# Spacing a router's serial search wider along a stream of matmuls

## The chip, the cores and the metric

The kernel runs on one core of one Trainium2 chip. The metric is the device time of one execution in microseconds (us). TensorE (PE) multiplies, VectorE (DVE), ScalarE (ACT) and GpSimd (POOL) do the elementwise work, and transfers are issued from the queues of SyncE (SP), ScalarE and GpSimd.

## What is computed

Attention over four batches of 576 tokens gives 2304 rows of 512 values. A dense layer follows, and then a mixture of eight experts in which each expert takes exactly 288 tokens, chosen greedily by descending gate value:

```python
a = x @ w1; b = x @ w2
x = (a * b @ w3) @ w_out                  # 2304 x 512
logits = x @ w_gate                       # 2304 x 8
order = np.argsort(-logits.flatten())     # greedy: best pairs of token and expert first
for idx in order:                         # skip a token that has an expert, an expert with 288 tokens
    ...
for e in range(8):
    h = np.maximum(x[mask_e] @ w1[e], 0)  # 512 -> 1024
    out[mask_e] = h @ w2[e]               # 1024 -> 512
```

Products run as three passes over a high and a low part of each operand (hh, hl, lh), so each product of the formula is three matmuls.

## The kernel before

The order on every engine is the order in which the program emits instructions; no scheduler reorders them. An engine works through its instructions in that order and stops at the first whose operands are not there. Four stages follow each other: attention with the first dense products (to about 304 us), the product w3 @ w_out (`make_w`, 8 tiles of 8 groups), x2 (`make_x2`, 18 chunks of 128 tokens, 8 groups each), and the experts.

Routing runs through the last three. It doesn't need x2, since the gate is folded into earlier weights. It has seven rounds; each round finds, by a search in six steps, the threshold at which some expert is full, gives that expert its tokens, and closes it. A step is a chain from engine to engine: VectorE compares all gate values with 40 trial thresholds (`Gt`, L808), TensorE counts with 18 small matmuls (L822) against a comparison matrix `CR` that ScalarE copies in two parts ahead of each round (L790), and VectorE picks the threshold (L824 to L827). Ahead of each round and behind it stand some 25 small VectorE operations and one pair of matmuls (L838, L840). After round k the index of the full expert (`wi`) is ready, and `make_list(k)` makes that expert's token list while round k+1 runs; its matmuls (L729, L730, L749) and routing's share one PSUM bank (tag `rt`).

`routing()` and the stream of other matmuls (`filler()`: x2, then the experts) are two generators. Where routing yields, it names how many ns it wants filled. The loop at the end gives the stream that many ns times a pace, and the stream pays per yield: 680 for three matmuls of 512 columns in x2, 395 for three of 288 columns in the experts. The pace is PACE0 while the stream is in x2 and PACE1 once it is in the experts. What a yield overshoots is carried over:

```python
for ns in route:
    want += ns * (PACE0, PACE1)[phase[0]]
    while want > 0:
        got = next(fill, 0)
        want = want - got if got else 0
```

A step asks 1050 (HALF_NS) and then 1700 (STEP_NS, 1550 for a round's first); a round asks 29,500 in all, routing 224,200. When routing has ended, the rest of the stream runs without a break.

Three other things lie in the stream. In x2, chunk c is copied out at chunk c+1 (`xout`): ScalarE copies it to `xr`, of which there is one buffer, and writes it to DRAM from its own queue (L617, L618). At the start of chunk c the operand of chunk c+2 is split (`gsplit`: ScalarE L502, L505, and an accumulating transfer from GpSimd's queue, L507). From chunk 8 on the weights of the first expert are loaded (`w_gather`, SP), from chunk 10 on they are split (`w_split`: ScalarE L942, L943 or L948; for one kind of weight an accumulating transfer, for the other subtractions). While routing runs, those subtractions are done on VectorE in quarters ("bites", L967); when it has ended, on VectorE in one or on GpSimd (L124).

The first expert's rows are special: the last two chunks come from on-chip copies (`X1`, L989), all others by three gathers from DRAM on GpSimd's queue (`first_rows`, L978), which wait for the write of chunk 15; TensorE places them by small matmuls (L998). For expert k+1 the rows are gathered at the third of the eight hidden blocks of expert k (L1025), and there the stream yields nothing until that expert's list exists. `hid` is L1047 to L1049, `yacc` L1071 to L1073.

Of the kernel before, what the change touches and what calls it, by code (L numbers as in the profile page):

```python
# [40 lines left out]

TAIL = 6

PACE0, PACE1 = 1.0, 1.3
STEP_NS, FIRST_NS, LIST_NS, SUM_NS, CR_NS, SMALL_NS, HALF_NS, COPY_NS, LATE_NS = 1700, 1550, 1800, 1800, 650, 1150, 1050, 900, 1500


# [1174 lines left out]
```

## Time and profile before

| what | us |
|---|---|
| median of 3 runs | 727.43 |
| lowest, highest | 726.01, 731.74 |
| the profiled execution | 728.83 |
| its span, first to last instruction | 727.0 |
| TensorE busy | 700.0 (96%) |
| VectorE, ScalarE, GpSimd busy | 409.8, 353.6, 265.6 |

All views below are of the one profiled execution. A matmul's end is modelled and drawn later than the start of the next, so the time that TensorE loses is read from starts. A timeline row merges equal instructions; its last bracket is the idle time ahead of it and what ended it.

### The profile page before, as it was taken

What the parts mean: (1) busy time and instruction counts of PE and PEld (TensorE: products, weight loads), DVE (VectorE), ACT (ScalarE), POOL (GpSimd) and SP (SyncE); (2) the same over time, 40 slices, a digit from 0 to 9 for tenths busy, and PEclk for the clock granted to TensorE, in tenths of its full rate; (3) what the DMA queues carried; (4) which work ended last, traced back from release to release, by engine and by line L of the source; (5) the groups of instructions that cost most, each with busy time, mean ns of one, the idle gap of its engine ahead of it and who ended that gap; (6) DMA issues with size and microseconds to landing.
All of it is one profiled execution on the core that took longest, in us unless ns stands there. A gap on an engine that the chain in (4) does not pass through costs nothing.

```text
span 727.0 us, 15967 instructions
## 1 busy us (share of the span) xinstructions
PE 700.0 (96%) x6081; PEld 610.0 (84%) x6081; DVE 409.8 (56%) x1414; ACT 353.6 (49%) x812; POOL 265.6 (37%) x305
## 2 busy tenths in 40 slices
PE   5799999999999999999999999999999999999996
PEld 3589778888889988687787878799998999999995
DVE  4879777773321111177785767678787863234321
ACT  5666445555422123332545464346575656655432
POOL 2858412321100035334345353421414145664521
PEclk9999999999999999999999999999999999999999
DMA  9995697971114200110799999768888797996311
GB/s 299 333 292 165 228 348 273 328 266 58 38 64 169 98 20 1 64 59 10 125 143 137 175 146 223 145 203 215 263 218 242 187 291 209 284 276 192 115 33 33
DMA packets 59596, 126.66 MB, mean 174 GB/s; under 512 B 13696, under 2 KB 29440, under 8 KB 56960
## 3 DMA queue, kind: packets, MB, share of 16 engines
q1 hardware_dynamic: 27232, 89.46, 36.7%
q0 software_dynamic: 29696, 31.46, 25.9%
q10 hardware_dynamic: 2592, 4.72, 1.9%
q8 instruction: 48, 0.79, 0.4%
q14 instruction: 28, 0.23, 0.1%
HBM read 87.87 MB, written 15.73 MB: 142 GB/s over the span
## 4 chain that ended last, share of the span: by engine, by line
PE 78%; issue 6%; DMA 6%; DVE 4%; POOL 3%; ACT 3%; POOLq 0%; SPq 0%; ACTq 0%; DVEq 0%
PE ps_ab L477 9%; PE ps_ab L478 9%; PE ps_ab L479 8%; PE ps_h L1047 4%; PE ps_ab L623 4%; PE ps_ab L1073 4%; PE ps_ab L1071 4%; PE ps_h L1049 3%; PE ps_h L1048 3%; PE ps_ab L1072 3%; PE ps_ab L624 3%; PE ps_ab L625 3%; PE ps_rt L822 2%; DMA qk<-qk_dram 2%; PE ps_rt L228 2%
## 5 line engine op out<-in xcount | busy, mean ns | idle before, releaser
L207 POOL TENSOR_TENSOR p<-p,sm 128x384 f32<-128x384 f32 x36 | 45.8, 1282 | 120.3 <-DVE sm L205 74.1
L1071 PE MATMUL ps_ab<-hh,w 128*128 128x288 f32 x248 | 76.2, 307 | 0.0
L1073 PE MATMUL ps_ab<-hh,w 128*128 128x288 f32 x248 | 73.1, 295 | 0.0
L1072 PE MATMUL ps_ab<-hl,w 128*128 128x288 f32 x248 | 73.0, 294 | 0.0
L507 POOL DMA_DIRECT2D wbl<-g x36 | 48.4, 1675 | 63.6 <-ACT wbl L505 54.6
L1060 DVE SCALAR_TENSOR_TENSOR hl<-ps_h,hh 128x288 fp32r<-128x288 f32 x62 | 28.2, 455 | 70.3 <-ACT hh L1059 61.8
L1059 ACT ACTIVATE hh<-ps_h 128x288 fp32r<-128x288 f32 x62 | 25.5, 412 | 85.7 <-PE ps_h L1049 76.4
L200 ACT ACTIVATE p<-p,sm 128x96 f32<-128x96 f32 x144 | 52.0, 363 | 24.2 <-DVE sm L193 23.3
L482 ACT ACTIVATE a<-ps_ab 128x512 f32<-128x512 f32 (+1 forms) x44 | 22.9, 521 | 80.7 <-PE ps_ab L479 73.8
L623 PE MATMUL ps_ab<-Wx,wbh 128*128 128x512 f32 x144 | 59.6, 414 | 0.0
L625 PE MATMUL ps_ab<-Wx,wbl 128*128 128x512 f32 x144 | 56.2, 391 | 0.0
L624 PE MATMUL ps_ab<-Wx,wbh 128*128 128x512 f32 x144 | 56.2, 390 | 0.0
L477 PE MATMUL ps_ab<-x,wah 128*128 128x512 f32 (+1 forms) x144 | 54.8, 381 | 0.7 <-ACT x L251 0.7
L477 PE MATMUL ps_ab<-x,wbh 128*128 128x512 f32 (+1 forms) x144 | 54.5, 378 | 0.0
L478 PE MATMUL ps_ab<-x,wah 128*128 128x512 f32 (+1 forms) x144 | 53.4, 371 | 0.1
L479 PE MATMUL ps_ab<-x,wbl 128*128 128x512 f32 (+1 forms) x144 | 53.2, 370 | 0.0
L479 PE MATMUL ps_ab<-x,wal 128*128 128x512 f32 (+1 forms) x144 | 53.2, 370 | 0.0
L478 PE MATMUL ps_ab<-x,wbh 128*128 128x512 f32 (+1 forms) x144 | 53.2, 369 | 0.0
L484 DVE TENSOR_TENSOR g<-a,ps_ab 128x512 f32<-128x512 f32 (+1 forms) x36 | 22.4, 623 | 53.3 <-PE ps_ab L479 50.4
L1072 PEld LDWEIGHTS ps_ab<-hl,w 128*128 128x128 f32 x248 | 46.7, 188 | 0.1
L1071 PEld LDWEIGHTS ps_ab<-hh,w 128*128 128x128 f32 x248 | 46.7, 188 | 0.0
L1073 PEld LDWEIGHTS ps_ab<-hh,w 128*128 128x128 f32 x248 | 46.5, 188 | 0.0
(296 smaller groups left out, 2042.8 us busy)
## 6 DMA issues: line engine op xcount, KB each, us to landing
est<-e_dram SPq DMA_DIRECT2D x53, 512.0 KB, 4.8
w<-w_dram SPq DMA_DIRECT2D x16, 1024.0 KB, 7.5
qk<-qk_dram SPq DMA_DIRECT2D x36, 320.0 KB, 4.5
w<-est POOLq DMA_DIRECT2D x20, 512.0 KB
wbl<-g POOLq DMA_DIRECT2D x28, 256.0 KB
v<-v_dram SPq DMA_DIRECT2D x36, 192.0 KB, 6.8
kept<-f SPq DMA_DIRECT2D x12, 512.0 KB, 4.1
rows<-e_dram SPq DMA_DIRECT2D x11, 512.0 KB, 5.8
```

The source lines that it names most:

```text
L200: act(p[:, i, :], p[:, i, :], AF.Exp, bias=sm[:, 1, i:i + 1], scale=-1.0, accum_out=sm[:, 2, i:i + 1])
L207: nc.gpsimd.tensor_tensor(p, p, sm[:, 3, :, None].to_broadcast([128, 4, KB]), op=OP.mult)
L477: mm(a, wh[:, k, fs], xh[:, k, ts], start=(k == 0), stop=False)
L478: mm(a, wh[:, k, fs], xl[:, k, ts], start=False, stop=False)
L479: mm(a, wl[:, k, fs], xh[:, k, ts], start=False, stop=(k == 3))
L507: nc.gpsimd.dma_start(x, src, accum_op=OP.add)
L623: mm(a, h[:, f, :], wh, start=(f == 0), stop=False)
L624: mm(a, h[:, f, :], wl, start=False, stop=False)
L625: mm(a, l[:, f, :], wh, start=False, stop=(f == 7))
L1071: mm(y, wh[:, f % 2, ds_], h, start=(f == 0), stop=False)
L1072: mm(y, wh[:, f % 2, ds_], l, start=False, stop=False)
L1073: mm(y, wl[:, f % 2, ds_], h, start=False, stop=(f == end))
```

## The change

Two constants: the stream gets 1.15 times (before 1.0 times) what routing asks while it is in x2, and 1.4 times (before 1.3 times) in the experts. No instruction is added or removed by it directly; the order in which both generators' instructions are emitted changes, and with it which weights are split while routing is still running.

```diff
-PACE0, PACE1 = 1.0, 1.3
+PACE0, PACE1 = 1.15, 1.4
 STEP_NS, FIRST_NS, LIST_NS, SUM_NS, CR_NS, SMALL_NS, HALF_NS, COPY_NS, LATE_NS = 1700, 1550, 1800, 1800, 650, 1150, 1050, 900, 1500
```

## Rows read from the trace of the kernel before

**Rows 1.** The page: span, TensorE and its weight loads, granted clock in 40 slices.

```profile
span 727.0 us, 15967 instructions
PE 700.0 (96%) x6081; PEld 610.0 (84%) x6081; DVE 409.8 (56%) x1414; ACT 353.6 (49%) x812; POOL 265.6 (37%) x305
...
PEclk9999999999999999999999999999999999999999
```

**Rows 2.** Busy time by stage: x2, then the experts while routing runs.

```profile
core 0: us, PE busy (x) PEld busy (x) DVE busy (x) ACT busy (x) POOL busy (x), PEclk, DMA share, GB/s
...
356.20:474.30 118.10, 116.32 (x903) 92.54 (x900) 85.74 (x331) 60.96 (x87) 54.14 (x43) 1.00 0.97 155
...
480.40:600.30 119.90, 117.16 (x1109) 114.78 (x1109) 94.51 (x341) 73.91 (x115) 35.30 (x45) 1.00 0.84 229
```

**Rows 3.** TensorE's waits from 305 to 602 us: total, times, longest.

```profile
PE ps_rt L822 <- ACT r_CR L790: 1.6, 1, 1.6
PE ps_rt L749 <- DVE r_tj L824: 1.2, 1, 1.2
PE ps_rt L838 <- DVE r_CGE L831: 1.1, 1, 1.1
PE ps_rt L822 <- DVE r_Gt L808: 0.7, 1, 0.7
PE ps_rt L749 <- DVE OH L744: 0.3, 1, 0.3
PE ps_rt L822 <- DVE r_lf L751: 0.2, 1, 0.2
```

**Rows 4.** TensorE in order of time (start, us): steps with a wait and without.

```profile
328.11 0.39 PE L594 MATMUL ps_ab<-wah,wbl 128*128 128x512 f32 x1
329.20 0.61 PE L822 MATMUL ps_rt<-r_Gt,r_CR 128*128 128x40 bf16 x18 [0.70 <-DVE r_Gt L808]
...
425.10 0.62 PE L822 MATMUL ps_rt<-r_Gt,r_CR 128*128 128x40 bf16 x18
...
426.35 0.39 PE L623 MATMUL ps_ab<-Wx,wbh 128*128 128x512 f32 x1
...
427.03 0.39 PE L623 MATMUL ps_ab<-Wx,wbh 128*128 128x512 f32 x1
...
428.40 0.62 PE L822 MATMUL ps_rt<-r_Gt,r_CR 128*128 128x40 bf16 x18
...
456.40 0.32 PE L822 MATMUL ps_rt<-r_Gt,r_CR 128*128 128x40 bf16 x6
458.28 0.47 PE L822 MATMUL ps_rt<-r_Gt,r_CR 128*128 128x40 bf16 x12 [1.56 <-ACT r_CR L790]
```

**Rows 5.** ScalarE in order of time, late in x2.

```profile
451.38 0.60 ACT L617 ACTIVATE xr<-ps_ab 128x512 f32<-128x512 f32 x1 [4.82 <-DMA x_d<-xr]
...
454.39 1.06 ACT L505 ACTIVATE wbl<-wbh 128x1024 fp32r<-128x1024 f32 x1
...
457.40 0.82 ACT L790 ACTIVATE r_CR<-r_Cc 128x768 bf16<-128x768 bf16 x1
...
462.89 0.60 ACT L617 ACTIVATE xr<-ps_ab 128x512 f32<-128x512 f32 x1 [2.72 <-DMA x_d<-xr]
463.52 0.33 ACTq L618 DMA_DIRECT2D x_d<-xr  x1
```

**Rows 6.** Line L618, the writes of x2's chunks: issue to landing.

```profile
DMA to landing us min/median/max: 2.6/5.8/8.3
```

**Rows 7.** GpSimd's gathers of expert 0's rows, and TensorE around them.

```profile
468.69 1.25 POOL L978 DMA_INDIRECT rows<-x_d,li  x1 [7.85 <-DVE r_lf L753]
...
471.53 1.20 POOL L978 DMA_INDIRECT rows<-x_d,li  x1 [0.30 <-issue]
...
459.83 0.39 PE L625 MATMUL ps_ab<-Wx,wbl 128*128 128x512 f32 x1
...
475.50 1.10 PE L998 MATMUL ps_h<-dg,rows 96*128 96x96 f32 x6
476.44 0.23 PE L822 MATMUL ps_rt<-r_Gt,r_CR 128*128 128x40 bf16 x3
```

**Rows 8.** Line L1025, the other experts' gathers: duration, first and last start.

```profile
L1025 POOL DMA_INDIRECT rows<-x_d,li x21: 919/932/1430, 483.8 to 672.3; - x21
```

**Rows 9.** Line L822, the search's matmuls: duration, first and last start.

```profile
L822 PE MATMUL ps_rt<-r_Gt,r_CR x756: 179/179/196, 318.4 to 565.4; 128*128 128x40 bf16 x189
```

## The prediction

> **What bounds the kernel now.** I read the page first, then the table by stage, then TensorE's waits, then the order of time around each wait, and last the queues behind the longest ones. The page [rows 1] shows TensorE busy for 96% of the span, and the granted clock at nine tenths or more (the page's highest digit) in every slice, so the clock is not in question. The stages that the change touches, x2 and the experts up to the end of routing, are as full: 116.32 of 118.10 us and 117.16 of 119.90 us [rows 2]. A busy matmul hides small gaps, since each is drawn at 0.39 us while the next one starts 0.23 us later; so I use starts. Three x2 matmuls take 0.68 us (426.35 to 427.03), and two steps of routing's search in an undisturbed stretch stand 3.30 us apart (425.10 to 428.40) [rows 4]: four groups of three, 2.73 us, and 0.57 us for the step's own 18 small matmuls.
>
> So all that wider spacing can win is the time in which TensorE stands at a routing matmul. The list of its waits [rows 3] has six, 5.1 us together. Each hides about 0.17 us more under the drawn end of the matmul before it, so about 6.1 us: in x2 1.7 (458.28 after its neighbour at 456.40, of which 0.14 is the six matmuls between), 0.86 (329.20) and 0.37, 2.9 together [rows 3, 4]; among the experts 1.4, 1.3 and 0.4, 3.1 together [rows 3]. That is 0.8% of the span. The other 39 of the 42 steps wait for nothing in that list, and more space gives them nothing.
>
> **What the change does to the order.** It removes and adds no instruction but moves routing's steps along the stream of other matmuls. A group of three x2 matmuls pays 680 of the grant, and a step asks 1050 + 1700 = 2750 ns: four groups at 1.0. At 1.15 it asks 3162, or 4.65 groups, so steps take four and five groups in turn. x2 with its matrix product has 64 + 144 groups and 4.05 us of the first expert's input: 145.5 us of grants, 2.0 of them given before routing starts. Routing asks 1.5 us and then 29.5 us a round. Before, x2 lasts to 143.4 us of routing's count, which includes all six steps of its fifth round (127.1 to 140.8); the count agrees with the trace, where a routing step still follows at 476.44, just after 475.50 [rows 7]. After, x2 lasts to 143.4 / 1.15 = 124.7 us of that count: the fifth round's six steps move into expert 0. The rest, 224.2 - 124.7 = 99.5 us, times 1.4, is 139 us of expert grants instead of 80.8 x 1.3 = 105, so routing ends as expert 5 starts and no longer late in expert 3 (an expert is 28.1 us).
>
> **Cost by cost.** The moved small matmuls themselves cost 0.57 us a step wherever they stand, 42 steps before and after: nothing.
>
> The 0.86 us wait [rows 4] belongs to the first round's fourth step. By the count it gets five groups instead of four, 0.68 us more: gain 0.68. The 0.37 us wait on a list's copy goes, since a step now asks 0.41 us more: gain 0.37.
>
> The 1.7 us wait is ScalarE's [rows 5]: the second copy of the round's comparison matrix (457.40) stands behind a chunk's split (to 455.36) and a weight copy, because a chunk started between the two copies. By the count no chunk at which weights are split starts between the two copies of any round after the change: chunk 12 starts before both, some 6 us of grants ahead of the step. I take the whole 1.7; if ScalarE is still behind there, nothing.
>
> Together x2 gains 2.8 us (bounds 0 and 2.9, the low one where the collisions recur at other steps).
>
> Now the loss. The first expert's rows are fetched by three gathers (POOL, L978) from x2 rows in DRAM. They wait for the write of chunk 15, issued after its copy on ScalarE at 462.89 (write at 463.52); the gathers are issued at 468.69 to 471.53 and TensorE uses them from 475.50, where it loses a few tenths at most before the step at 476.44 [rows 5, 7]. So from that copy to the last row is about 13.3 us, and today TensorE arrives just then. Chunk 15's last matmul starts at 459.83 [rows 7], and from there to 475.50, 15.7 us, TensorE has its own 0.23, 16 groups (10.9 us), eight 288-column matmuls (by columns 288/512 of 0.23 us each, 1.0) and, in the remaining 3.5 us, four search steps of 0.57 us and a list's four small groups. After the change that stretch holds one step and one sum pair (0.57 and, put at most at the same, 1.1 us together) in place of the 3.5, because the fifth round moves out: TensorE arrives about 2.4 us sooner. The chain of copy, write and gathers isn't shortened by that. ScalarE's copy came 2.7 us after chunk 15's end (460.2 to 462.89), since the one buffer xr is free only when the previous write has landed: the wait before 451.38 was 4.82 us, and landings took 2.6 to 8.3 us [rows 5, 6]. Chunks 10 to 12 get no step after the change and pass in about 5.5 us each, less than the 5.8 us of a median write, so ScalarE won't catch up. The stall before the last rows is then the lag less about 0.2 us: 0 if ScalarE has no lag, 4.6 with the 4.82 us seen. I take the lag of before: +2.4 us. What is late next is only expert 0's input, and all queues behind it shift alike.
>
> A rule of the Trainium skill speaks against that loss. "DMA: Bandwidth & Descriptors", section "Queues, rings and completion order", says that each DMA engine takes turns between its queues packet by packet. By it ScalarE's 256 KB write would not be held back by POOL's accumulating transfers, and the sum would be 2.4 us less. The row with landings of up to 8.3 us for one and the same write [rows 6] leaves that open at best.
>
> Among the experts, 18 steps stand instead of 12. At today's rate (3.1 us over 12) six more cost 1.5 us; the wider stretches ahead of the three waits (1800 x 0.1 = 0.18 us ahead of a sum, 0.1 to 0.17 ahead of the others) take off 0.4. But the waits are coincidences with a row gather on POOL rather than a rate, and the first one (483.8 [rows 8]) now meets the fifth round. I take +0.6, bounds -3.1 and +1.5.
>
> Five weight pieces (those of experts 4 and 5 that before come after routing's end) are now subtracted in quarters on VectorE, four of them instead of on POOL. VectorE is busy 94.51 of 119.90 us in the stage where it has routing as well [rows 2] and has less beside it later: nothing. Two edges I counted for lateness: expert 6's list is complete about 19 us of grants before its gather and its index about 24 us before its first load, so no list or weight holds the fill.
>
> **Sum.** -2.8 + 2.4 + 0.6 = +0.2 us. The profiled execution took 728.83 us (span 727.0 and 1.8 around it), so 729.0 by its own measure; it lies 1.4 us above the median of three, 727.43, which gives 727.6. The likeliest case's own range is 726 to 729.
>
> **Rivals.** First, the rows are there in time (the write lands early, or as the rule has it): -2.8 + 0 + 0.6, or with the experts' waits unchanged -2.8: 724.6 to 725.2. For it speaks the least landing, 2.6 us; against it the lag on three chunks in a row. Chance 0.27.
>
> Second, slower: the gathers are late by more. One place, L998, and one mechanism: the write of chunk 15 waits for chunk 14's. With a lag of 4.82 us the stop is 4.6 and the sum -2.8 + 4.6 + 0.6 = +2.4: 729.8. With the experts' upper bound 730.7. It decides from a lag of 2.4 us upwards; for 1% it would need about 9.7, two slow writes one behind the other. Chance 0.20.
>
> Third, the experts' waits all go, as the wider grants are meant to do: -2.8 + 2.4 - 3.1 = -3.5: 723.9. Against it: 0.1 to 0.18 us more per stretch against waits of over 1 us. Chance 0.08.
>
> The forecast has 0.41. The 0.04 left is for a miss in the counts, a list or weight that is late after all.
>
> **Range and chances.** From 723.0 to 732.0: below lies only the case in which nothing new appears and all six waits go (727.43 - 6.1 = 721.3), above only two slow writes or a missed list. About 1%, 7.3 us, is what a measurement of this kernel can tell from no change. Faster than that needs more than the 6.1 us there are to win, and the runs shown spread by 5.7 us: 0.04. Slower by 1% needs the lag of 9.7 us or a late list: 0.07. Within: 0.89.
>
> **What would show it.** Right: the last x2 steps gone from before 475, the first expert matmul (L1047) 4 to 5 us earlier than before (six steps of 0.57 us, a list's groups and the net of x2's gain and loss), the wait on the comparison matrix (L822 on L790) gone, a stop of 1 to 4 us at L998 on the rows, the last search step 139 - 105 = 34 us of grants later, near 600 us instead of 565 us [rows 9], and waits at L838 and L749 still there. Wrong: no stop at L998 (first rival); a stop of over 5 us there; or waits on weights or lists in experts 4 to 6, which would mean that the counts of grants are wrong.

## The result and the profile after

| | before | after |
|---|---|---|
| median (us), 11 runs each | 727.26 | 730.07 |
| lowest, highest | 724.97, 731.74 | 728.34, 735.37 |
| the profiled execution, its span | 728.83, 727.0 | 728.41, 726.6 |
| ratio after to before, 95% interval | | 1.0055 [1.0037, 1.0073] |

The change made the kernel about 0.55% slower: within the 1% that was called "no change", but not nothing. (The ratio, here and below, compares all runs of the two kernels; it is not the quotient of the two medians, which is 1.0039.) The profiled execution of after is one of its two shortest, 1.7 us under its own median, and that of before lies 1.6 us above its own. So these two traces show no loss between them, the spans being 727.0 and 726.6; they show what went and what came. A second trace of after, in the fifth experiment, is 3.8 us longer than that of before.

The page of after (span, TensorE, granted clock in 40 slices), which answers to [rows 1]:

```profile
span 726.6 us, 15962 instructions
...
PE 701.3 (97%) x6081; PEld 612.3 (84%) x6081; DVE 414.6 (57%) x1433; ACT 353.5 (49%) x812; POOL 252.9 (35%) x289
...
PEclk9999999999999999999999999989999999999999
```

One slice is no longer at the top digit. GpSimd has 12.7 us less and VectorE 4.8 us more: the weight pieces that moved, as counted.

TensorE's waits from 305 to 602 us of after, the same view as [rows 3]: total, times, longest. It is the whole list.

```profile
PE ps_h L998 <- DMA rows<-x_d,li: 2.8, 3, 1.3
```

Before it had six entries, none of them this one. All six are gone, and one has come. TensorE in order of time around it (start, us; merged rows; idle before and what ended it):

```profile
455.46 0.40 PE L625 MATMUL ps_ab<-Wx,wbl 128*128 128x512 f32 x1
...
468.68 0.30 PE L989 MATMUL ps_ab<-oh,wbl 128*128 128x288 f32 x1
469.75 0.46 PE L998 MATMUL ps_h<-dg,rows 96*128 96x96 f32 x2 [0.77 <-DMA rows<-x_d,li]
471.02 0.46 PE L998 MATMUL ps_h<-dg,rows 96*128 96x96 f32 x2 [0.81 <-DMA rows<-x_d,li]
472.74 2.02 PE L998 MATMUL ps_h<-dg,rows 96*128 96x96 f32 x8 [1.26 <-DMA rows<-x_d,li]
474.56 2.77 PE L998 MATMUL ps_ab<-dg,rows 96*128 96x96 f32 x12
477.03 0.59 PE L989 MATMUL ps_h<-oh,wbh 128*128 128x288 f32 x1
...
478.62 0.44 PE L989 MATMUL ps_ab<-oh,wbh 128*128 128x288 f32 x1
478.86 0.33 PE L989 MATMUL ps_ab<-oh,wbl 128*128 128x288 f32 x1
479.03 0.30 PE L1047 MATMUL ps_h<-x,wah 128*128 128x288 f32 x1
```

The first row is the last matmul of chunk 15. TensorE stops three times at L998, once for each gather; with the part that hides under drawn ends it loses 0.94, 0.97 and 1.42 us, 3.3 together. And then the same matmuls run slower: L989, started every 0.13 us ahead of the stop, now starts every 0.24 us. The table by stage (columns as in [rows 2]) says why:

```profile
core 0: us, PE busy (x) PEld busy (x) DVE busy (x) ACT busy (x) POOL busy (x), PEclk, DMA share, GB/s
354.45:468.68 114.23, 114.19 (x830) 91.11 (x829) 73.97 (x289) 60.40 (x86) 52.40 (x41) 1.00 1.00 159
470.00:480.00 10.00, 7.93 (x40) 7.60 (x40) 2.11 (x8) 3.18 (x6) 3.13 (x8) 0.66 0.92 320
479.03:602.00 122.97, 122.94 (x1230) 120.40 (x1229) 101.60 (x353) 76.86 (x119) 34.36 (x43) 1.00 0.84 222
```

From 470 to 480 us the granted clock is 0.66 on the mean, which is 6.8 us at 1.2 GHz instead of 2.4. Ahead of the stop TensorE is busy for 114.19 of 114.23 us, among the experts for 122.94 of 122.97: the wider spacing did there what it says. Everything lost lies in the 10 us between.

Where the rows come from, by the chain that ended last, in order of time (start, us, what):

```profile
425.13 5.44 DMA x_d<-xr
431.28 7.34 DMA x_d<-xr
439.33 10.38 DMA x_d<-xr
450.43 5.45 DMA x_d<-xr
456.60 4.17 DMA x_d<-xr
461.48 4.13 DMA x_d<-xr
466.33 2.01 DMA x_d<-xr
469.21 3.49 DMA rows<-x_d,li
```

From 425 to 466 us the end of the kernel hangs on one buffer: six times a chunk's copy waits until the write before it has landed. (The write of 466.33 is chunk 16's, which the gathers don't need; that link is only inferred by the view.) ScalarE says the same (as [rows 5] and [rows 6] of before):

```profile
449.80 0.60 ACT L617 ACTIVATE xr<-ps_ab 128x512 f32<-128x512 f32 x1 [6.90 <-DMA x_d<-xr]
...
460.85 0.60 ACT L617 ACTIVATE xr<-ps_ab 128x512 f32<-128x512 f32 x1 [2.82 <-DMA x_d<-xr]
```

```profile
DMA to landing us min/median/max: 2.0/4.8/10.4
```

Chunk 15 is copied at 460.85, 5.0 us behind the end of its last matmul (455.46 and 0.40). Before, that lag was 2.7 us. Last, the search ends where the count put it (compare [rows 9]):

```profile
L822 PE MATMUL ps_rt<-r_Gt,r_CR x756: 179/179/196, 320.0 to 597.6; 128*128 128x40 bf16 x189
```

**The account of the two profiled executions**, by starts. From the first matmul of w3 @ w_out to the first of expert 0 (L1047) it took 174.4 us before (305.98 to 480.42) and 172.7 after (306.29 to 479.03). The three waits that went give -2.95; the stop +3.3; the half clock +3.0 (from the first L998 to L1047 9.28 us here, without the later two stops 6.89; the same 24 and 8 matmuls take 3.88 at the full clock in the third experiment, without its stops). That leaves -5.1 for what moved out: six steps of 0.57, 3.4, and the small matmuls of a list and of a sum. From L1047 to the last matmul it took 239.05 and 240.02 us: 5.1 moved in, and 3.6 of waits gone (1.38, 1.29, 0.43, 0.25 and 0.25), +1.5 worked out, +1.0 measured. Together -0.7 here, and -0.4 in the spans.

### The profile page after: what moved, and what is told of

It is laid out like the page before. It is cut to its first block, busy times and chain, and to the rows that moved or that the text cites. A ratio compares the mean times of both kernels' runs of the same rounds, so it can differ in the third digit from the quotient of the medians.

```text
span 726.6 us, 15962 instructions
## 1 busy us (share of the span) xinstructions
PE 701.3 (97%) x6081; PEld 612.3 (84%) x6081; DVE 414.6 (57%) x1433; ACT 353.5 (49%) x812; POOL 252.9 (35%) x289
## 4 chain that ended last, share of the span: by engine, by line
PE 80%; DMA 8%; issue 5%; ACT 3%; POOL 2%; DVE 2%; POOLq 0%; SPq 0%; ACTq 0%; DVEq 0%
PE ps_ab L477 9%; PE ps_ab L478 9%; PE ps_ab L479 9%; DMA x_d<-xr 5%; PE ps_h L1047 4%; PE ps_ab L1071 4%; PE ps_h L1049 4%; PE ps_h L1048 4%; PE ps_ab L1072 4%; PE ps_ab L1073 4%; PE ps_ab L623 3%; PE ps_ab L625 3%; PE ps_ab L624 3%; PE ps_rt L822 2%; PE ps_rt L228 2%
## 5 line engine op out<-in xcount | busy, mean ns | idle before, releaser
L507 POOL DMA_DIRECT2D wbl<-g x36 | 48.6, 1686 | 61.1 <-ACT wbl L505 52.7
L625 PE MATMUL ps_ab<-Wx,wbl 128*128 128x512 f32 x144 | 56.4, 391 | 0.0
L944 POOL DMA_DIRECT2D w<-est x20 | 21.3, 1066 | 83.0 <-ACT w L943 32.6
L1071 PEld LDWEIGHTS ps_ab<-hh,w 128*128 128x128 f32 x248 | 46.8, 189 | 0.0
```

The costliest lines, as they stand in the source:

```text
L507: nc.gpsimd.dma_start(x, src, accum_op=OP.add)
L625: mm(a, l[:, f, :], wh, start=False, stop=(f == 7))
L1071: mm(y, wh[:, f % 2, ds_], h, start=(f == 0), stop=False)
```

## The experiments

All ratios are against the kernel before, run on the same chip beside it; the experiments ran on several chips. "x2 1.15" and "experts 1.4" stand for PACE0 and PACE1.

**1. The spacing in x2 alone.**

```diff
-PACE0, PACE1 = 1.0, 1.3
+PACE0, PACE1 = 1.15, 1.3
```

> The wider pace in x2 alone (1.15 and 1.3). Theory A (the rows of expert 0 come late, and the granted clock falls behind that stop): both stay, and the experts' waits at L838 and L749 come back, up to 3 us: 730 to 733, with a stop of 2 to 4 us at L998. Theory B (what costs is that routing reaches further into the experts): routing ends earlier than in the changed kernel, so it is faster than that, 727 to 729.

Measured 734.23 us against 729.43, ratio 1.0060 [1.0038, 1.0082]. The stop at L998 is there (0.82, 0.97, 1.20 us), the half clock behind it too, and among the experts four waits are back (0.63, 1.46, 0.32, 0.77). So the loss goes with the spacing in x2, and the waits among the experts go only with 1.4. The time lies above the 730 to 733 of theory A, and it can't be told from that of the changed kernel (1.0055, and 1.0059 in experiment 5): with 1.15 and one buffer, 1.4 among the experts takes the waits away but no time that these runs resolve. Why isn't shown; the trace of experiment 5 has 3.4 us more of half clock at the end of x2 and just behind it than this one.

**2. The spacing among the experts alone.**

```diff
-PACE0, PACE1 = 1.0, 1.3
+PACE0, PACE1 = 1.0, 1.4
```

> The wider pace in the experts alone (1.0 and 1.4). Theory A: x2 and the join to expert 0 are as before, no stop of over 0.5 us at L998 and no fall of the clock there, and the experts' waits (3.1 us) go: 723 to 726, faster than before. Theory B: routing still reaches further into the experts than before, so slower than before, 728 to 730.

Measured 726.29 against 729.43, ratio 0.9949 [0.9929, 0.9968]: half of the change is a gain of 0.5%. No stop at L998. Its profiled execution, one of its longest (729.64), loses in x2, at the wait on the comparison matrix that the old order has too [rows 4], but now longer. TensorE in order of time, then the 10 us behind it with the granted clock:

```profile
456.74 0.32 PE L822 MATMUL ps_rt<-r_Gt,r_CR 128*128 128x40 bf16 x6
460.01 0.47 PE L822 MATMUL ps_rt<-r_Gt,r_CR 128*128 128x40 bf16 x12 [2.95 <-ACT r_CR L790]
```

```profile
460.00:470.00 10.00, 9.99 (x80) 7.73 (x81) 6.65 (x27) 2.09 (x3) 2.58 (x3) 0.83 1.00 153
```

A stop of another kind at another place, and behind it again a fall of the clock, 3.4 us at 1.2 GHz (0.83 over 10 us).

**3. The changed kernel with two buffers for the copied rows.** From chunk 12 on every other chunk is copied to a second buffer, so a copy no longer waits for the write just before it.

```diff
-            r = pm.tile([128, D], F32, tag="xr", name="xr", bufs=1) if late < 1 else rows0[0][:, 3 * D:4 * D]
+            r = rows0[0][:, 3 * D:4 * D] if late >= 1 else slot(9, [128, D], F32, "xr") if c >= 12 and c % 2 == 0 else pm.tile([128, D], F32, tag="xr", name="xr", bufs=1)
```

> The changed kernel with a second buffer for the copies of x2's chunks 12, 14 and 16, so that ScalarE's copy of chunk 15 does not wait for the landing of chunk 14. Theory A, chain of one buffer: ScalarE's lag at chunk 15 falls from 5.0 us to under 1, the stop at L998 from 3.1 to under 1 us, the clock stays at 2.4 GHz there, 724 to 727. Rival: the writes land late because of GpSimd's accumulating transfers, not because of the buffer; then ScalarE's copy is early but the stop stays at 2 to 3 us, and the time at 729 to 731.

Measured 725.95 against 729.43, ratio 0.9941 [0.9920, 0.9962], the lowest of all, though those of experiments 2 and 7 lie in its interval. ScalarE in order of time, then the first two of TensorE's waits from 305 to 640 us, then the stretch from 440 to 500 us with the granted clock:

```profile
448.61 0.60 ACT L617 ACTIVATE xr<-ps_ab 128x512 f32<-128x512 f32 x1 [1.57 <-PE ps_ab L625]
...
455.40 0.60 ACT L617 ACTIVATE xr<-ps_ab 128x512 f32<-128x512 f32 x1 [1.14 <-PE ps_ab L625]
```

```profile
PE ps_h L998 <- DMA rows<-x_d,li: 0.7, 1, 0.7
PE ps_ab L625 <- ACT wbh L614: 0.7, 1, 0.7
```

```profile
440.00:500.00 60.00, 58.31 (x511) 51.48 (x510) 43.94 (x155) 26.95 (x41) 16.43 (x19) 1.00 0.90 204
```

ScalarE now waits for TensorE instead of a write: chunk 15's copy starts 0.04 us behind its last matmul. Stops of 0.9 us each (by starts) are left at L998 and at L625, and the clock is full from 440 to 500 us. (The stop at L625 ended at 462.87, and the copy of L614 that the view names had ended at 462.31; experiment 5 says what ended it.) The writes themselves are no faster (4.1/7.0/8.8 us to landing, against 2.0/4.8/10.4), so it was the one buffer that made the rows late, not the speed of a write.

**4. The changed kernel with 16 more matmuls of 512 columns ahead of L998**, 3.6 us of work that fills the stop; their product is not used.

```diff
+PAD = 16
...
+        pad = bank([128, MAIN], "tr")
+        h0, l0 = GS[NC - 1]
+        wh0 = Wx[3][0][:, 1, :]
+        for n in range(PAD):
+            mm(pad, h0[:, 7, :], wh0, start=(n == 0), stop=(n == PAD - 1))
```

> The changed kernel with 16 more matmuls of 512 columns (3.6 us at 2.4 GHz, result not used) put where TensorE stands waiting for expert 0's rows. If it is the stop that takes the clock down (theory A), the added work fits into the 3.1 us stop, the clock stays at 2.4 GHz there, and the time is 2 to 4 us below the changed kernel, 726 to 728. If the clock falls for another reason, it still falls and the time is the same or up to 2 us more, 730 to 732.

Measured 731.9 against 729.43, ratio 1.0028 [1.0004, 1.0053]. TensorE in order of time (lines behind 625 are shifted by one to six, so L626 is L625 and L1004 is L998):

```profile
465.56 0.47 PE L626 MATMUL ps_ab<-Wx,wbl 128*128 128x512 f32 x1 [2.35 <-issue]
...
473.31 3.84 PE L1001 MATMUL ps_tr<-Wx,wbh 128*128 128x512 f32 x16
476.99 1.47 PE L1004 MATMUL ps_h<-dg,rows 96*128 96x96 f32 x12
478.30 1.50 PE L1004 MATMUL ps_ab<-dg,rows 96*128 96x96 f32 x12
```

Twelve L998 matmuls follow without a stop and take 1.3 us where the second twelve took 2.5 in the changed kernel: the clock is full there. That a stop was filled is seen beside experiment 5, the same kernel without the padding: TensorE came to this place 0.6 us sooner there (472.67 against 473.31), the last gather was issued 0.5 us sooner (471.81 against 472.33), TensorE stopped for 1.8 us, and 6.8 us at half clock followed. So the clock does as theory A says. The time does not: 731.9 lies in the range of the other theory, 730 to 732, and not in 726 to 728. With 3.6 us of work put in, the kernel was still no slower than the changed one (the intervals overlap, so a gain isn't shown), but another stop appears, of 2.5 us, earlier, at the third matmul of the first group of chunk 17, with 3.4 us of half clock behind it.

**5. The changed kernel once more**, on another chip.

> The changed kernel once more, on the same chip as the next three and with a second profile; its first profiled execution (728.41 us) lies 1.7 us below its median. Theory A: stops of 2.5 to 4 us at L998 and of 0.2 to 2.5 us at the low part of chunk 17's operand (L625), a stretch of 7 us or more at 1.2 GHz behind them, none among the experts; slower than before by 0.3 to 0.7%. Theory B (the cost is among the experts): waits of over 2 us in the fifth to seventh round.

Measured 733.61 against 728.73, ratio 1.0059 [1.0038, 1.0080]. TensorE in order of time, then the granted clock:

```profile
464.93 0.47 PE L625 MATMUL ps_ab<-Wx,wbl 128*128 128x512 f32 x1 [2.27 <-issue]
...
473.77 0.46 PE L998 MATMUL ps_h<-dg,rows 96*128 96x96 f32 x2 [0.74 <-DMA rows<-x_d,li]
474.97 1.13 PE L998 MATMUL ps_h<-dg,rows 96*128 96x96 f32 x8 [0.74 <-DMA rows<-x_d,li]
```

```profile
460.00:470.00 10.00, 7.72 (x27) 5.95 (x26) 5.29 (x25) 1.79 (x3) 2.18 (x3) 0.83 0.89 146
470.00:480.00 10.00, 8.52 (x47) 7.88 (x46) 2.15 (x8) 3.59 (x6) 2.33 (x7) 0.81 0.77 261
480.00:490.00 10.00, 10.00 (x96) 9.78 (x95) 8.13 (x27) 5.64 (x9) 3.83 (x4) 0.85 0.40 125
```

Here the order of the instructions is the same as in the first trace of after, but TensorE stops twice: at L625 for 2.4 us, and at L998 for 1.8. Each time the clock falls behind it, for 3.4 and for 6.8 us. In the first trace the stop at L625 was 0.2 us. What L625 waits for there is the accumulating transfer of L507 that writes the low part of chunk 17's operand. Its last part was issued at 454.94 in the first trace of after and at 457.77 here; its last landing is recorded at 462.57 and at 464.84, each 0.09 us before that matmul starts, and it is so in experiments 1, 3, 4 and 12 too. That is one way to the spread of one and the same kernel from 728 to 736 us: transfers that land a little later or earlier decide which stop there is, and the clock adds to it. Two traces don't show that it is the only one.

**6. The old order, with the gathers put into GpSimd's queue one chunk later.**

```diff
-                if f == 2 and c == NC - ONE:
+                if f == 2 and c == NC - 1:
```

> The kernel before with only the issue of expert 0's three gathers moved from chunk 16 to chunk 17 (8 groups of x2 later), so that TensorE stops at L998 in the old order of steps too. Theory A: the gathers land some 3 to 5 us later than they are needed; the clock falls to 1.2 GHz behind that stop, so the kernel loses more than the stop itself: 4 to 9 us above before. If the clock does not follow a stop, it loses 3 to 5 us with the clock at 2.4 GHz.

Measured 729.18 against 728.73, ratio 1.0003 [0.9984, 1.0023], and no stop: a miss. The gathers wait for chunk 15's write anyway, so it doesn't matter where behind it they are put. It does say that the place in the queue isn't what binds.

**7 and 8. Two buffers with x2 1.0 and experts 1.4, and with the old 1.0 and 1.3** (edits as in 3 and 2).

> Pace 1.0 in x2 and 1.4 in the experts, with the second buffer of chunks 12, 14 and 16. Theory A: x2 keeps its 0.9 us and 0.4 us waits, but ScalarE is not late at the fifth round's comparison matrix (1.7 to 3.1 us), no stop at L998, no waits of over 1 us among the experts: 0.5 to 0.9% faster than before, at least as fast as with the experts' pace alone. If the buffer is not what makes ScalarE late there, as with the experts' pace alone: 0.4 to 0.6% faster.

> The kernel before (1.0 and 1.3) with only the second buffer of chunks 12, 14 and 16. Theory A: the wait of L822 on L790 in the fifth round (1.7 us and more in slow executions) goes and nothing else, so 0.2 to 0.5% faster than before. Rival: ScalarE was late because of its own queue, and the wait stays: no difference.

Measured 726.46 and 727.62 against 728.73: ratios 0.9955 [0.9935, 0.9975] and 0.9980 [0.9961, 1.0000]. In neither does TensorE wait for the comparison matrix: with the copies on time ScalarE has done it when it is wanted. A stop of 1.0 and of 0.4 us appears at L998 instead, since TensorE comes there sooner. Among the experts experiment 8 has the waits of before (L749 1.1, L838 1.0, L749 0.3 in its list; compare [rows 3]), experiment 7 none over 0.5 us. On time experiment 7 can't be told from experiment 2, which has one buffer (0.9949): at 1.0 the second buffer takes away a wait, but no time that these runs resolve, and the 0.5 to 0.9% expected of it isn't shown.

**9. The old spacing, with the gathers made to wait for chunk 16's write as well**: a stop at L998 without the change. The edit of experiment 6 goes with it.

```diff
-            nc.gpsimd.indirect_dma_start(out=x[:KB, D * j:D * j + D], out_offset=None, in_=x2_d[:128 * (NC - ONE), :],
+            nc.gpsimd.indirect_dma_start(out=x[:KB, D * j:D * j + D], out_offset=None, in_=x2_d[:128 * (NC - ONE + 1), :],
```

> The kernel before with its old spacing (1.0 and 1.3); its three gathers of expert 0's rows are made to wait for the write of chunk 16 as well, one chunk later than they need, and are issued one chunk later. Nothing else is changed and no work is left out. It makes a stop at L998 without the wider spacing. Theory A (a stop in the stream of matmuls at this place is followed by a stretch at half the granted clock, whatever made the stop): a stop of 4 to 7 us at L998 in the old order, the clock at 1.2 GHz for 3 to 7 us behind it, and so 6 to 10 us over the kernel before, ratio 1.008 to 1.014. Theory B (the half clock belongs to the wider order of steps and not to the stop): the same stop, the clock full behind it, 4 to 7 us over, ratio 1.005 to 1.010. The clock in the record tells them apart, not the time.

Measured 737.86 against 729.6, ratio 1.0084 [1.0052, 1.0117]. TensorE's wait at L998 from 305 to 640 us, and the granted clock behind it:

```profile
PE ps_h L998 <- DMA rows<-x_d,li: 2.5, 3, 0.9
```

```profile
480.00:490.00 10.00, 8.26 (x53) 7.69 (x53) 2.55 (x12) 1.98 (x5) 3.15 (x8) 0.58 0.86 306
490.00:500.00 10.00, 10.00 (x71) 10.00 (x70) 7.86 (x32) 6.35 (x9) 0.98 (x1) 0.91 0.35 76
```

By starts the stop is 3.0 us, less than the 4 to 7 that both theories put there: the first gather was issued at 476.6, only 2.9 us behind the issue of chunk 16's write (473.7), which it now waits for. But the clock falls, for 10.2 us (8.4 and 1.8), longer than the 3 to 7 expected. So the fall belongs to the stop and not to the wider order. Of the 10.5 us by which this span, the longest of the five, exceeds that of before, 2.9 lie ahead of w3 @ w_out and have nothing to do with the edit.

**10 and 11. A smaller step: x2 1.05, experts 1.4, with one buffer and with two.**

> Spacing 1.05 in x2 (instead of 1.15) and 1.4 in the experts; one buffer for the rows as before. By the count three of the six steps of the fifth round still stand ahead of the first expert's rows, so TensorE comes to L998 later than in the changed kernel by about 1.7 us (three steps of 0.57 us). Theory A (the loss in x2 is the stop at L998 and the half clock behind it): a stop of 0.8 to 1.8 us instead of 3.1, the clock full or low for no more than 3.4 us, and 725.5 to 728 on a chip where the kernel before takes 728, ratio 0.996 to 1.000. Theory B (the loss goes by the spacing in x2 itself): a third of what 1.15 cost over 1.0, some 2.5 us over the kernel with 1.0 and 1.4, ratio 0.998 to 1.001.

> Spacing 1.05 and 1.4, and from chunk 12 on two buffers in turn for the copied rows. Theory A (with two buffers the rows are no longer late by much, so what the spacing in x2 costs is gone): no stop over 1 us in x2, no half clock between 440 and 500 us, the waits among the experts gone or under 0.8 us each, ratio 0.992 to 0.996, as 1.15 with two buffers. Theory B (the loss goes by the spacing in x2): better than 1.15 with two buffers by about 2 us, ratio 0.990 to 0.992.

Measured 732.99 and 732.02 against 729.6: ratios 1.0047 [1.0028, 1.0066] and 1.0029 [1.0012, 1.0046]. Both expectations fell, of both theories. The stop at L998 did as it was told (one of 0.7 us, and none), but other waits came. TensorE's waits of experiment 11 from 305 to 640 us:

```profile
PE ps_ab L625 <- DMA wbl<-gt: 2.3, 1, 2.3
PE ps_ab L1072 <- DVE r_lf L751: 1.4, 1, 1.4
PE ps_rt L749 <- DVE r_tj L824: 1.3, 3, 0.6
PE ps_h L1047 <- DVE x L1004: 1.0, 1, 1.0
PE ps_rt L822 <- DVE r_Gt L808: 0.7, 1, 0.7
PE ps_tr L1098 <- ACT rows L1100: 0.7, 1, 0.7
PE ps_rt L729 <- DVE r_Acl L723: 0.7, 1, 0.7
```

8.1 us in one list, with the same 1.4 among the experts that left nothing over 0.5 us in experiment 7. In experiment 10 the entries among the experts are the same ones at the same lines (L749 1.1, L1047 1.0, L729 0.7, L1098 0.7), and in x2 the wait on the comparison matrix is back with 1.7 us and 3.4 us of half clock behind it. Shifting routing by a fraction of a chunk places every later step elsewhere; what it meets there is not read off the spacing. The first line also names the transfer at L625 that the views of experiments 4 and 5 left unnamed: the accumulating transfer of L507. Here it was issued at 451.27 and TensorE went on at 466.08.

**12. x2 1.15, experts 1.3, with two buffers**, the fourth corner.

> Spacing 1.15 in x2 and the old 1.3 in the experts, with two buffers for the copied rows: it closes a square with 1.0 and 1.3, 1.0 and 1.4, and 1.15 and 1.4, all with two buffers (ratios 0.998, 0.9955 and 0.9941). Theory A (what is left to win in x2, once the rows come in time, is the waits at routing's steps there, some 1 to 2 us, and it is won by the spacing in x2 alone): 1.5 us under 1.0 and 1.3 with two buffers, ratio 0.995 to 0.9965. Theory B (in x2 the waits only change their places; the gain is that of 1.4 among the experts): the same four waits among the experts as with 1.15 and 1.3 and one buffer, 3.2 us together, and as much lost in x2 as with 1.0 and 1.3, ratio 0.997 to 1.000.

Measured 727.15 against 729.59, ratio 0.9969 [0.9953, 0.9984], between the two ranges; the interval covers both, so it doesn't decide between them. The profile has both effects: the waits among the experts are those of experiment 1 (0.62, 1.38, 0.31, 0.78), as the second theory has it, and up to L1047 it loses as much as experiment 8: 1.6 us (1.2 at L625 and 0.4 at L1047, against 0.9, 0.4 and 0.4). The four corners with two buffers:

| | experts 1.3 | experts 1.4 |
|---|---|---|
| x2 1.0 | 0.9980 | 0.9955 |
| x2 1.15 | 0.9969 | 0.9941 |

Going to 1.4 is worth 0.25 and 0.28%, 1.8 to 2.0 us of 728; going to 1.15 is worth 0.11 and 0.14%, about 1 us, less than the intervals. (The four ratios come from three chips.)

## Why the prediction was right, and where it was not

The time lies in the range and on the side of "no change", but 1 us above the likeliest case's own range, 726 to 729, and the sum of +0.2 us came out of terms that were off on both sides. In the two traces they are -2.95 (waits in x2), +3.3 (stop), +3.0 (clock) and -3.6 (experts), -0.2 together: two large errors, the last two, nearly cancel, and that is luck. What the median has above that is not in these two traces; experiment 5 shows one form of it, the stop at L625. Point by point:

**The counts of grants held.** Six steps went from x2 into expert 0, the last search step starts at 597 us where "near 600" stood, no list and no weight holds the stream. But the first expert matmul came only 1.7 us sooner (counted from the first matmul of w3 @ w_out) and not 4 to 5: the clock, 3.0, and the longer stop, 0.9, took the rest.

**The three waits in x2: right**, in place and in size (2.8 forecast, 2.95 gone). But experiment 8 shows that 1.7 of it, the wait on the comparison matrix, goes as well with a second buffer at the old spacing. It was a result of ScalarE's late copies rather than of too little space; experiment 2 has it at 3.1 us by starts and experiment 10 at 1.8.

**The stop at L998: right in place, cause and size** (2.4 forecast, 1 to 4 as the bounds of what would show it, 3.3 measured), but its terms were not. The lag was taken as that of before, 2.7 us. It was 5.0, as in the second rival; that chunks 10 to 12 would pass faster than a write lands was said, and not drawn to its end: a lag that can't be caught up grows. That the whole was only 0.9 over the forecast is because the way from the copy to the last row took 11.9 us (460.85 to 472.74) and not 13.3.

**The rule of the Trainium skill** ("DMA: Bandwidth & Descriptors", section "Queues, rings and completion order": each DMA engine takes turns between its queues packet by packet) was weighed as a rival in which the rows come in time. They did not. The longest write, issued at 439.33, took 10.4 us. In the stretch from 439 to 450 us the view of the DMA queues of after shows GpSimd's queue (q0) and ScalarE's (q10) as a share of 16 engines' span:

```profile
q0 software_dynamic: 1558, 1.40, 95.3%
...
q10 hardware_dynamic: 144, 0.26, 8.7%
```

The write of 466.33, with a DMA share of 0.36 around it, landed in 2.0 us. These rows don't speak against turns; they show that turns beside a queue that keeps the engines busy are no guarantee of a short landing.

**The step that failed: the waits among the experts.** The prediction gave them +0.6 us, called them coincidences with a gather, and put 0.08 on all of them going. All went: -3.6. Experiments 2 and 7 show that this is the effect of 1.4 at the twelve steps that were there, and the wait list of after that the six new steps brought none. The argument from 0.1 to 0.18 us more per stretch against waits of over 1 us did not hold. A likely reason, which no run shows by itself, is that the grants also move each step against the gather that it met, and the sum of the earlier grants (0.1 x 29.5 = 3 us in every round) moves it far more than the stretch just ahead of it. That place counts as well as space is what experiments 10 and 11 say, where 1.4 left such waits at four lines and at five.

**What was missing altogether: the clock.** That "the clock is not in question" was read from the page of before. It was in question as soon as a stop was forecast: 6.8 us at 1.2 GHz cost 3.0 us, nearly as much as the stop itself (3.3). Experiment 9 shows it in the old order. Nor was the stop at L625 foreseen, which costs up to 2.5 us and another stretch of half clock. ScalarE's lag can bring it, since the split of a chunk's operand stands behind the late copy in ScalarE's queue. But experiment 11 has it with no such lag, and in experiment 3 the last part of that transfer was issued 11 us sooner than in experiment 5 (446.79 against 457.77) and still landed only at 462.78, 16.0 us later, against 7.1 us there. So the lag is not the only cause; what makes the transfer slow stays open.

Of the rivals, the second (rows later, 729.8 to 730.7) is nearest to the median of 730.07, but not for its reason alone: the third happened at the same time, and the clock took back what it gave. The first was wrong in after; experiment 3 comes near it, with 0.9 us of stop left at L998.

## What to carry to other kernels

When a change makes the main engine arrive earlier somewhere, work out what it arrives at, follow that chain back to the first resource that it really waits for (here one buffer, six writes earlier) and widen that in the same edit: the same spacing was 0.55% slower with one buffer and 0.6% faster with two. (1.4 among the experts alone, with one buffer, was already 0.5% faster.) A stop of a few us on TensorE is to be priced with the half clock that can follow it, not only with its own length. And a spacing between two serial chains is not a dial with a slope: with two buffers 1.05 was worse than 1.0 and than 1.15, so try a few values and read the list of waits of each.

## What the runs showed of the hardware

The granted clock fell from 2.4 to 1.2 GHz behind stops of the matmul stream of quite different causes: rows from a gather (after, experiments 1, 5 and 9), a matrix copied by ScalarE (2 and 10), an operand from an accumulating transfer (4 and 5). It stayed at 2.4 GHz behind the 1.7 us wait of before [rows 4] and the stops of 0.9 to 1.0 us in experiments 3 and 7. The size alone doesn't decide: behind 1.8 us in experiment 10 it fell, and behind 2.5 us at L625 in experiment 11 it did not. Nor does it decide how long the half clock lasts: 3.4 us behind a stop of 3.1 us in one piece (experiment 2), 10.2 us behind 3.0 us in three pieces (experiment 9). What decides is left open.

The writes of 256 KB at L618, all alike, took from 2.0 to 10.4 us to land within one execution of after. The last part of chunk 17's accumulating transfer took 7.1 us in experiment 5 and 16.0 us in experiment 3.
